# A transformer block with segment memory on one core: token blocks 1 to 3 in one load, a re-annealed instruction list, and other value columns in the memory products of heads 20 to 31

## The chip, the core and the metric

The kernel runs on one core of one Trainium2 chip. The metric is the device time of one execution in microseconds (us). Before the change it is 297.37 us, the median of 3 runs (297.17 to 298.87). One further execution was taken with the profiler; its own time is 295.65 us, of which the profile shows a span of 293.9 us from the first to the last instruction.

The engines have short names here: PE multiplies matrices (PEld loads its weights), ACT evaluates functions and copies, DVE and POOL do elementwise work, and SP issues the transfers (DMAs). Each engine works through its own instructions strictly in order and waits for the others by semaphores.

## The reference

Input `x` has 2048 tokens of 640 features in bf16; there are 32 heads of 20 features and 4 segments of 512 tokens.

```python
def _A_ref(x, wq, wk, wv, wo, beta):          # H = 32, Dh = 20, N = 4, L = 512
    q, k, v = ...                              # x @ wq, x @ wk, x @ wv, cut into heads and segments
    phi = lambda t: jnp.where(t > 0, t + 1.0, jnp.exp(t))
    g = _sigmoid(beta)
    for s in range(N):
        p = _softmax(einsum(qs, ks) * scale + mask)      # causal inside the segment
        a_dot = einsum(p, vs)
        a_mem = einsum(phi(qs), M) / (einsum(phi(qs), z) + 1e-06)
        outs.append(g * a_mem + (1.0 - g) * a_dot)
        M = M + einsum('bhld,bhle->bhde', phi(ks), vs)   # memory: phi(k) of a head times v of the same head
        z = z + einsum('bhld->bhd', phi(ks))
    return o @ wo

h  = x + _A_ref(_layernorm(x), ...)
h2 = h + silu(_layernorm(h) @ w1) @ w2         # w1 640x1728, w2 1728x640
```

## The kernel before

The 2048 tokens are 16 blocks of 128 (numbered 0 to 15), and four blocks are one segment. `build` declares several hundred small tasks for each segment, and each task emits one or a few instructions on one engine. A task's name says what it does. The names that matter later are:

- `x0`, `x1`, `x2`, `x4`, `x8`, `x12`: loads of token blocks by `load_x` (L581), named after their first block; `w_q0`, `w_q1`, `w_k0`, `w_k1`, `w_wv`: the weights of the projections in raw order (L584); `w_wo`, `w_w1_c`, `w_w2_k`: later weights.
- `n1_stB`, `n1_rsB`, `n1_apB`: the first layer norm of block B: statistics on DVE (L753, L756) or on ACT in five instructions (L744 to L748); the reciprocal root on POOL (L763, L765); and the scaling on DVE (L781) or, for block 0, possibly on ACT (L777). For blocks 0 to 3, `n1_tpB` transposes on PE (L791) and `n1_teB` copies the result out on ACT (L800); later blocks are transposed by a DMA (`n1_trB`, L806).
- `re_wqC`, `re_wkC`: copies that put the raw weights of column group C into head order (L711), on DVE, POOL or ACT; group 0 is in two halves, the second one with an `h` at the end.
- `prSCW`: projection of segment S, group C, to q (W=0) or k (W=1) on PE (L548, or L549 for the variant in four column tiles, marked `/C` in the list). `qeSCW` copies it out (L876 on ACT, L877 on DVE). Group 0 of segment 0 is split in token halves x and y.
- `exSCW`, `paSCW`, `pbSCW`: the feature map phi on ACT and DVE (L883, L890, L896).
- `vSB`, `veSB`: the values of a block and their copy (L842 on ACT, L843 on DVE).
- `vtSN`: twelve small DMAs per segment that gather the features of groups 5 to 7 (L908).
- `qkTa`, `qkTb`, `qkTe`: scores of tick T (segment T div 8, head group T mod 8) in PSUM (L946); `eT..` their exponentials on ACT (L959, two for each score task); `mkT..` the causal mask on POOL (L971); `avT` probabilities times values (L994); then `oeT`, `tdT`, `tmT`, `nmT`, `adT` (scaling, transposing, memory read, division, sum).
- `ktSC`, `mzSC`, `mbSC`: the memory update: phi(k) transposed by DMA (L1101), its products with the values (L1112), and the masked copy.
- `otB`, `woB`, `rsB`: attention output transposed, multiplied by `wo`, added to x (L1161, L548, L1176); `n2_...B`: second layer norm; `h1_S_F`, `thS_F`, `sS_F`, `h2_B`, `oB`, `outB`: the feed-forward part (L548/L1198, L1211, L1217, L548, L1254, L1259).

What sets the order is one text, `ORDER`: a list of about 1460 entries, of the form `name/engine:slots`. `Graph.schedule` walks through it, gives each task its engine and its buffer slots (PSUM banks 0 to 7, rotating SBUF buffers), and emits it. So the list fixes the order of work on each engine and on SP's queue. A `Tracker` adds the semaphore waits that the data and the buffers need. Eight PSUM banks are shared by all tasks: a later user of a bank waits for the copy that empties it.

The loads are declared with a first block, a count, a priority and a bandwidth figure; only the first two have an effect on what is emitted:

```python
load_x(0, 1, -100, 2.30, "fix", (SP,))
load_x(1, 1, -99, 2.33, "fix", (SP,))
...
load_x(2, 2, -97, 4.79, "fix", (SP,))
```

A load has one semaphore, so a task that needs any block of a load waits for the whole load.

In the memory update each group C holds heads 4C to 4C+3 in its first 20 rows and parts of heads 20 to 31 in its other rows. One product multiplies phi(k) of such a row block with the values of two or three heads at once, and a mask keeps what belongs together. The masks (`blk_head`) take block 1 to heads 20 to 23, block 3 to heads 24 to 27 and block 5 to heads 28 to 31.

Of the kernel before, what the change touches and what calls it, by code (L numbers as in the profile page):

```python
# [368 lines left out]
qe021/D:0 e0a0 pr010.0:6 vpad2 w_w1_0/S pa021:1 n1_st4:3 pr010.1 qe010/D pa011:2 n1_st5:0 ex011:1 pb011 kt01:3  # L369
qk0b0:4,2 w_w1_2/S e0b2:5 e0b0 v00.0/C:0 pr020.0/C:7 pr020.1/C mk0a qe020/A v00.1/C n1_rs5 vt09:0 zf0 vt03 n1_st7:1  # L370
n1_rs7 qk0e0:2,4 v01.0:6 v01.1 e0e2:2 v02.0:4 e0e0 ve01/D:0 zf1 v02.1 n1_ap5:0 n1_tr5:2 ve00/A vt00 qk1a0:6,1 ex021:1
pr031.0:3 pr031.1 ve02/D n1_st6:7 lsc0 e1a0:1 n1_rs4 n1_ap4:1 e1a2 qe031/D:0 qk1b0:6,4 v03.0:0 lsc1 lsc2 lsc3
pr041.0:2 e1b0:6 pr041.1 x8/S:8,9,10,11 v03.1 e1b2 qe041/D:0 ex031:0 qk2a0:4,6 n1_tr4 mm5 mk0e pa041:2 n1_rs6 n1_ap6:2
n1_tr6 n1_ap7:3 ex041:2 mzc10 mm2 mk0b pr040.0:3 e2a0:3 mta3 pr040.1 pr030.0:2 ve03/D e2a2 qk2b0:4,0 e2b0:0 vt06
pr030.1/C qe040/D pa031:0 av0:3 pb021 mk1a qe030/D mm1 n1_tr7 vt05 oe0/D:0 qk2e0:6,4 vt010 mk1b av1:2 e2b2 epsg1 mk2b
pb041 mk2a td0/C:3 e2e2:5 e2e0 oe1/D:1 qk3a0:4,0 nm0:3,0 vt07 e3a2:6 v10.0:2 td1:6 nm1:2 vt011 e3a0 v10.1 ve10/D:1
qk3b0:0,6 e3b2:4 e3b0 mm7 n1_st9:2 mk2e av2:3 mk3a oe2/D:1 qk4a0:6,4 e4a2:3 v11.0/C:2 e4a0 v11.1/C qk4b0:0,4 td2/C:6
epsg0 ve11/D pb031 mk3b nm2:2 mtb3 av3:7 e4b0:1 vt01 e4b2 vt02 n1_rs9 oe3/D:0 mzc1 n1_st10:7 vt08 n1_st8:1 vt04
qk4e0:2,0 mk4a pr100.0/C:4 e4e2:4 pr100.1/C qe100/D:0 pa100:0 qk5a0:0,6 pr110.0/C:5 pr110.1/C e4e0 qe110/D:0 e5a0:5
w_wo/S:0 qk5b0:2,0 pr120.0/C:4 pr120.1/C qe120/D:0 mk4b e5a2 mk4e av4:5 oe4/D:1 mk5a kt02:0 pa120:0 e5b2:2 qk6a0:0,6  # L380
n1_rs8 td3/C:4 n1_ap8:0 nm3:0 e5b0 mk5b v12.0:2 v12.1 kt04:4 ve12/D e6a0:1 ex120:0 e6a2 w_w2_3/S td4:1 ex100:1 mz01:0
mz00 mm8 mz04 mz02 kt03:1 n1_rs10 n1_ap10:3 mz03 ma0/D:0 qk6b0:4,2 e6b2:0 e6b0 mk6b nm4:3 pr101.0:7 pr101.1 qk6e0:0,2
e6e2:6 qe101/D av5:6 pr111.0/C:7 pr111.1/C e6e0 qk7a0:4,2 mk6e w_w2_0/S mk6a e7a0:4 e7a2 n1_tr8:1 mk7a oe5/D:0 qe111/D
td5:6 pr130.0/C:0 pr130.1/C nm5:1 n1_tr10 qk7b0:6,4 e7b2:5 e7b0 mk7b n1_ap9:0 qe130/D:0 n1_st11:7 v13.0:1 mm3 v13.1/C
ve13/D ex101:2 n1_rs11 av6:0 qk8a0:3,6 e8a0:3 pa101:0 e8a2 pr140.0:5 pr140.1/C av7:4 oe6/D:1 mzc3 qk8b0:0,2 w_w1_4/S
td6/C:6 e8b0:2 w_w1_3/S n1_tr9 mzc5 pb101 kt10:1 qe140/D:0 oe7/D:0 mk8a nm6:2 pr131.0/C:7 td7/C:4 nm7:1 mzc7 mzc4
ot0:0 qk8e0:5,0 pr131.1/C ot1 n1_ap11:1 mm0 qe131/D pr121.0:4 pr121.1 pa130:0 pa110:0 ot2 qe121/D vt19:0 pa131:1 mzc0
e8b2 mk8b e8e0:5 w_w2_4/S mzc2 qk9a0:5,2 pb100 e8e2 mk8e pr141.0:7 pr141.1 qe141/D pa121:0 e9a2:4 qk9b0:0,2 e9a0 pb120
pa111:2 wo0.0/C:4 wo0.1/C rs0 e9b0:6 av8:7 e9b2 vt12 mk9b ot3 ex110:0 wo1.0/C:0 qk10a0:3,5 oe8/D:0 n1_tr11 vt16
n2_st0:1 vt10 e10a0:3 wo1.1 rs1 n2_st1:6 mb00:0 mm11 vt13 e10a2 wo2.0:2 wo2.1 rs2 ex111:2 pb111 n2_st2:0 mk10a  # L390
qk10b0:6,0 e10b2:0 vt11 wo3.0/C:4 wo3.1/C qk10e0:2,0 rs3 vt15 n2_rs1 e10b0 vt14 v21.0:6 e10e2:2 vt18 n2_ap1:0 n2_st3:6
e10e0 v21.1 ve21/D:0 mm9 qk11a0:4,0 e11a0:1 mm6 n2_tr1:0 v20.0/C:2 v20.1/C n2_rs0 v22.0/C:4 n2_rs2 tm8/C:6 td8/C
# [930 lines left out]
```

## Time and profile before

| what | value |
|---|---|
| median of 3 runs | 297.37 us (297.17 to 298.87) |
| the profiled execution's own time | 295.65 us |
| its span | 293.9 us |
| PE busy | 282.0 us (96%), 4365 matmuls |
| DVE, ACT, POOL busy | 218.6, 216.5, 148.1 us |
| chain that ended last, by engine | PE 83%, DVE 7%, ACT 6%, DMA 1%, issue 1% |
| granted PE clock | 9 tenths or more in each slice, mean 1.00 |

Busy time counts instructions on an engine. A share over the whole span mixes stages with different limits: the first 10 us have no projection yet, then scores and exponentials come first, and at the end only the feed-forward part is left. So the table is read together with the views by stretches of time.

### The profile page before, as it was taken

The page shows a single profiled execution, that of the slowest core. Times are in us where ns is not written, and L with a number is a line of the kernel's source. Part 1 is how long each engine was busy: PE and PEld are TensorE (multiplying, and loading weights), DVE is VectorE, ACT ScalarE, POOL GpSimd, SP SyncE. Part 2 cuts the span into 40 slices and gives each one's busy share as a digit, 9 for nine tenths or more (in the row PEclk, how much of TensorE's full clock was granted, in tenths as well). Part 3 has the DMA queues.
Part 4 walks back from the last instruction along what each step waited for, and adds up shares of the span by engine and source line. Part 5 has one row for each costly group of instructions (what it writes and reads, how often), then busy time and mean ns, then how long its engine had stood idle before and what let it go on. Part 6 is the DMA issues. An engine that isn't in the chain of part 4 may idle for free.

```text
span 293.9 us, 10138 instructions
## 1 busy us (share of the span) xinstructions
PE 282.0 (96%) x4365; PEld 159.8 (54%) x4365; DVE 218.6 (74%) x456; ACT 216.5 (74%) x281; POOL 148.1 (50%) x294
## 2 busy tenths in 40 slices
PE   6899889999999999999999899999999999999996
PEld 5454435445644445566654554656664657754574
DVE  3999888899997678798899835877746776635613
ACT  7699999999999899977789857979979640005400
POOL 6759675686947545746748432348638321300000
PEclk9999999999999999999999999999999999999999
DMA  7947869635464200453543402403320031450003
GB/s 212 342 120 186 113 176 186 167 69 108 87 80 113 73 2 3 53 99 70 91 122 92 93 2 21 81 2 57 73 25 2 2 70 22 91 156 0 3 0 112
DMA packets 48604, 24.83 MB, mean 84 GB/s; under 512 B 38896, under 2 KB 47472, under 8 KB 48560
## 3 DMA queue, kind: packets, MB, share of 16 engines
...
## 4 chain that ended last, share of the span: by engine, by line
PE 83%; DVE 7%; ACT 6%; DMA 1%; issue 1%; POOL 0%; SPq 0%; ACTq 0%; DVEq 0%
PE ps_all L548 49%; PE ps_all L549 20%; PE ps_all L946 8%; ACT PT L959 5%; PE ps_all L994 5%; DMA x_tok<-in_A_x_dram 1%; PE ps_all L1198 1%; DVE xn_rot L781 1%; DVE oTs L1010 1%; DVE phiQ L890 1%; DVE stt L753 1%; PE ps_all L1112 1%; DVE Vx L843 1%; DVE otok L1046 1%; DVE QK L877 0%
## 5 line engine op out<-in xcount | busy, mean ns | idle before, releaser
L959 ACT ACTIVATE PT<-ps_all 128x1024 bf16<-128x1024 f32 x160 | 154.1, 1027 | 16.2 <-PE ps_all L946 15.1
L971 POOL TENSOR_SCALAR_AFFINE_SELECT PT<-PT 128x512 bf16<-128x512 bf16 x128 | 82.8, 651 | 63.9 <-ACT PT L959 60.5
L1211 ACT ACTIVATE th<-ps_all 128x512 f32<-128x512 f32 (+1 forms) x56 | 31.7, 589 | 38.1 <-PE ps_all L548 23.7
L1217 DVE SCALAR_TENSOR_TENSOR sT<-th,ps_all 128x512 bf16<-128x512 f32 (+1 forms) x56 | 36.0, 661 | 17.0 <-ACT th L1211 16.4
L548 PE MATMUL ps_all<-w_sb,sT 128*128 128x320 bf16 x324 | 46.3, 299 | 0.1
L548 PE MATMUL ps_all<-tT,w_sb 128*128 128x512 bf16 x178 | 41.4, 380 | 0.0
L548 PEld LDWEIGHTS ps_all<-w_sb,sT 128*128 128x128 bf16 x324 | 31.0, 98 | 13.2 <-issue 0.6
L753 DVE BATCH_NORM_STATS2 stt<-x_tok 128x6 f32<-128x320 bf16 x62 | 27.1, 478 | 3.8 <-DMA x_tok<-in_A_x_dram 3.6
L1072 POOL TENSOR_TENSOR otok<-on 128x320 bf16<-128x320 bf16 x24 | 19.7, 824 | 17.5 <-DVE on L1064 17.5
L1254 DVE SCALAR_TENSOR_TENSOR x_tok<-ps_all,x_tok 128x640 bf16<-128x640 f32 (+1 forms) x17 | 13.3, 784 | 17.9 <-PE ps_all L548 13.1
L548 PEld LDWEIGHTS ps_all<-tT,w_sb 128*128 128x128 bf16 x178 | 16.5, 98 | 18.7 <-issue 0.6
L877 DVE CAST QK<-ps_all 128x512 bf16<-128x512 f32 x25 | 17.1, 685 | 8.6 <-PE ps_all L548 4.7
L1010 DVE TENSOR_SCALAR oTs<-ps_all,lsc 128x512 bf16<-128x512 f32 x26 | 19.3, 741 | 2.6 <-PE ps_all L994 2.2
L549 PE MATMUL ps_all<-tT,w_sb 128*32 128x512 bf16 x328 | 20.5, 380 | 0.0
L1064 DVE TENSOR_TENSOR on<-ps_all,rd 128x640 bf16<-128x640 f32 x24 | 19.8, 824 | 0.8
L765 POOL TENSOR_TENSOR rst<-rst,eps_c 128x1 f32<-128x1 f32 x32 | 18.3, 573 | 2.5
L549 PE MATMUL ps_all<-w_sb,sT 128*32 128x320 bf16 x496 | 18.8, 300 | 0.0
L781 DVE TENSOR_SCALAR xn_rot<-x_tok,mvt,rst 128x640 bf16<-128x640 bf16 x31 | 16.1, 534 | 3.3 <-POOL rst L765 2.8
L548 PE MATMUL ps_all<-tT,wkr 128*128 128x512 bf16 (+1 forms) x77 | 18.4, 367 | 0.0
L548 PE MATMUL ps_all<-wv_sb,tT 128*128 128x320 bf16 x115 | 18.0, 300 | 0.5 <-ACT PT L959 0.3
L763 POOL TENSOR_TENSOR rst<-mvt,eps_c 128x1 f32<-128x1 f32 x32 | 6.7, 209 | 22.5 <-DVE mvt L756 21.8
L994 PE MATMUL ps_all<-PT,Vx 128*32 128x512 bf16 (+3 forms) x384 | 17.4, 301 | 0.0
(111 smaller groups left out, 403.1 us busy)
## 6 DMA issues: line engine op xcount, KB each, us to landing
out_dram<-x_tok SPq DMA_DIRECT2D x15, 160.0 KB, 1.9
...
```

What stands on the lines that cost most here:

```text
L548: return [lambda e: e.matmul(out, lhsT=lhsT, rhs=rhs, start=start, stop=stop)]
L549: return [lambda e, p=p: e.matmul(out[p:p + 32, :], lhsT=lhsT[:, p:p + 32], rhs=rhs, start=start, stop=stop, tile_position=(0, p)) for p i ...
L753: T.add(DV, lambda e, hh=hh: e.bn_stats(out=stt[:, s, 6 * hh:6 * hh + 6], in_=xb[:, 320 * hh:320 * hh + 320]), reads=R((xa, xsub)), writes ...
L946: fns.append(lambda e, j=j, o=o, r=r, q0=q0, q1=q1, qa=qa, ka=ka: e.matmul(ps_all[:, o:o + q1 - q0], lhsT=ka[32 * r:32 * r + DH, 128 * j:1 ...
L959: T.add(AC, lambda e: e.activation(out=pt[:, pta.slot, q0:q0 + 2, 0:width], in_=sc3[:, b0:b0 + 2, 0:width], func=ACT.Exp, scale=SCALE), re ...
L971: fns.append(lambda e, v=v: e.affine_select(out=v, in_=v, pattern=[[0, 4], [1, 128]], compare_op=ALU.is_ge, fill=0.0, base=0, channel_mult ...
L994: fns.append(lambda e, j=j, r=r, h=h, pa=pa, pt=pt, co=co, q0=q0, ji=ji: e.matmul(bank(po)[32 * r:32 * r + 32, q0:hi], lhsT=vtile(vx)[:, j ...
L1010: f = lambda e: e.tensor_scalar(out=o, in0=i_, scalar1=lsc[:, g:g + 1], scalar2=None, op0=ALU.mult)
L1064: T.add(DV, lambda e: e.tensor_tensor(out=on[:, ona.slot, :, :].rearrange("p b (x e) -> p b x e", e=DH), in0=v[:, :, :, 0:DH], in1=r2.unsq ...
L1072: T.add(PO, lambda e: e.tensor_tensor(out=o_dst, in0=on[:, ona.slot, 0, :].rearrange("p (i x) -> p i x", i=4), in1=on[:, ona.slot, 1, :].r ...
L1211: T.add(AC, lambda e: e.activation(out=th[:, tha.slot, lo:hi], in_=bank(ps)[:, lo:hi], func=ACT.Tanh, scale=0.5), reads=R((ps, [0])), writ ...
L1217: T.add(DV, lambda e: e.scalar_tensor_tensor(out=sT[:, f, lo:hi], in0=th[:, tha.slot, lo:hi], scalar=1.0, in1=bank(ps)[:, lo:hi], op0=ALU. ...
```

## The change

There are three edits.

1. Blocks 1, 2 and 3 come in one load of 480 KB instead of one of 160 KB and one of 320 KB; the load `x2` is gone.
2. `ORDER` is another list for the same tasks (less `x2`).
3. In the memory products of groups 0 to 2, the value columns of the second head are 20 heads further on, not 16.

```diff
-    load_x(1, 1, -99, 2.33, "fix", (SP,))
+    load_x(1, 3, -99, 2.33, "fix", (SP,))
     load_w("wv", wv_sb[:, :, :], cw(A_wv), -98, 4.96, [(W["wv"], [0])], "fix", (SP,))
-    load_x(2, 2, -97, 4.79, "fix", (SP,))
...
-                heads = [(4 * c, 16, 2)] if c < 3 else [(12, 8, 3)] if c == 3 else [(16, 8, 2), (28, 1, 1)]
+                heads = [(4 * c, 20, 2)] if c < 3 else [(12, 8, 3)] if c == 3 else [(16, 8, 2), (28, 1, 1)]
```

The list, its first part (old, then new):

```diff
-epsc:0 iota halfc zpad warm:0 x0:0 mt2 n1_st0:4 mt3 mt0 mt1 mta1 mtb1 vpad1 x1:1 n1_st1/A:1,2 x2:2,3 w_q0:0 w_q1 w_k0
-vpad0 fill25:0 n1_rs0 n1_ap0/A:1 sel n1_tp0:2 fill5:7 n1_te0/A:1 n1_st2/D:5,3 mta0 n1_rs1 n1_st3:0 n1_rs2 w_k1 w_wv:0
-n1_rs3 re_wk4/G:0 mtb0 mm4 n1_ap1 n1_tp1:0 n1_ap2 n1_tp2:4 n1_ap3:0 n1_tp3:2 re_wq0/D:0 n1_te1/A pr000x.0:6 re_wq0h/D
-re_wk2/G pr000x.1 re_wk0/D re_wq2/D n1_te2/A n1_te3/A pr001x.0:5 qe000x/D:0 re_wk0h/D pr000y.0:4 re_wq3/G beta
-pr001y.0:0 x4/S:4,5,6,7 pr000y.1 qe000y/A w_w1_1/S:0 mta2 mtb2 mm10 pr001y.1 re_wk1/D re_wq1/D qe001y/A pr001x.1
-pr011.0:2 pr011.1 re_wk3/D qe001x/A re_wq4/G qk0a0:0,3 ex001:0 pa001:0 pb001 kt00:2 pr021.0:7 pr021.1 e0a2:4 qe011/D:0
...
+zpad:0 x0:0 mt0 epsc halfc n1_st0:4 iota sel x1:1,2,3 n1_st2/D:5,3 w_q0:0 w_q1 w_k0 mta0 n1_rs0 fill25:0 warm:0
+n1_st3:0 n1_st1/A:3,0 n1_rs1 w_k1 n1_ap1 n1_ap0/A:1 n1_tp0:2 fill5:7 re_wq0/D:0 n1_rs2 n1_ap2 n1_rs3 n1_tp1:4 n1_tp2:6
+n1_te0/A:0 re_wq0h/G n1_te1/A n1_ap3:2 n1_tp3:1 re_wk0/D:0 n1_te2/A pr000x.0:5 pr000x.1 qe000x/D:0 re_wk0h/G n1_te3/A
+pr001x.0:6 pr000y.0:0 pr000y.1 pr001y.0:4 pr001x.1 pr001y.1 re_wq4/A re_wk1/D qe001y/D qe000y/A re_wk2/D re_wq3/G mtb0
+pr011.0:7 pr011.1 re_wq2/G qe001x/A qk0a0:3,1 ex001:2 qe011/D:0 w_wv:0 beta re_wq1/G w_w2_5/S pa001:0 x4/S:4,5,6,7
+pr021.0:6 pr021.1 qe021/D:0 lsc0 lsc1 e0a2:3 re_wk4/G re_wk3/G w_wo/S:0 pr010.0:7 pr010.1 pb001 n1_st4:3 e0a0 ex011:0
+qk0b0:5,1 n1_rs4 mt2 pr020.0/C:3 qe010/D pr020.1/C mm9 vpad2 qe020/D vt03:0 x8/S:8,9,10,11 e0b2:2 v00.0/C:0 vt06 e0b0
...
```

Read by engine, the lists compare as follows.

- PE has the same 510 tasks in almost the same order: between two neighbouring score tasks stand the same tasks nearly throughout.
- With `/C` stand 30 of 84 `pr` tasks before and 36 after, 9 and 13 of 32 `v`, 33 and 31 of 108 `h1`, 18 and 9 of 65 `h2`, 13 and 8 of 32 `td`, 9 of 24 `tm` and 9 of 32 `wo` both times. The matmuls are 4365 before and 4209 after. Between neighbours in the list PE changes between full array, row tiles and column tiles 173 times before and 176 times after.
- ACT: `qe001y` and `qe020` go to DVE, `re_wq4` comes from POOL, `lsc0` stands ahead of the first exponential, and the load `w_w1_3` is issued from ACT's queue.
- POOL: `re_wq0h`, `re_wk0h`, `re_wq2`, `re_wq1` and `re_wk3` come from DVE; `re_wk2` goes to DVE. The constants `vpad0`, `vpad1`, `mt1`, `mt2`, `mt3` and their masks stand later. The first masks are in the order `mk0e`, `mk1a`, `mk0b`, `mk0a` instead of `mk0a`, `mk0e`, `mk0b`, `mk1a`, `mk1b`.
- DVE: `ve03` stands ahead of `pa041` and `n1_ap6`; `n1_ap8` stands after `ve12`; `n1_ap5` comes after `nm0`, much later than before.
- SP: `x2` is gone; `w_w2_5`, `w_wo` and `x8` come earlier, `kt00` and `kt01` later, and `n1_tr5` is the 27th transfer instead of the 18th (behind `vt08`, `vt07`, `vt010` and `vt00`, among others).
- The last norms of blocks 12 to 15 and the tasks around `wo13` are in another order: 9 PE tasks stand between `wo13.1` and the first `h1_3`, not 14.

More of the change, by code (lines that the diff above doesn't have):

```diff
@@ L368 @@
-pr011.0:2 pr011.1 re_wk3/D qe001x/A re_wq4/G qk0a0:0,3 ex001:0 pa001:0 pb001 kt00:2 pr021.0:7 pr021.1 e0a2:4 qe011/D:0
[L369 to L392, printed above, removed]
@@ new lines @@
+w_w1_2/S:0 n1_rs6 ex021:2 e1a0:6 qe031/D:0 qk1b0:4,6 n1_ap7:0 mm0 w_w1_4/S e1a2 mk1a v03.0:0 pr041.0:2 e1b2:1 mta2
+mtb2 pr041.1 qe041/D:0 mk0b v03.1 ve03/D n1_ap6:2 n1_tr7 e1b0 qk2a0:4,6 mk0a n1_tr6 ex031:0 pr030.0:2 ex041:1 pa041:0
+pr040.0:3 mk1b pr040.1 qe040/D e2a0:0 qk2b0:4,0 pr030.1 e2a2 qe030/D lsc3 e2b0:4 av0:3 vt08 mt1 vt07 e2b2 qk2e0:6,4
+e2e2:2 mm7 vt010 mta1 oe0/D:1 pb041 av1:2 oe1/D:0 mtb1 vt00 td0:3 nm0:2,0 n1_ap5:0 n1_tr5 vt02 mk2b qk3a0:4,0 v10.0:2
+e2e0 td1:7 nm1:0 vt05 v10.1/C ve10/D:1 e3a2:1 n1_st10:4 mt3 e3a0 vt011 pa031:2 pb031 mk2a vt04 qk3b0:0,6 mk2e av2:5
```

160 lines of the change are left out of this document (89 added, 71 removed).

## The prediction

> **What bounds the kernel now.** I read the page's busy line first, then the view of busy time by stretches (span, then PE, PEld, DVE, ACT, POOL, clock, DMA share, GB/s), cut where the limit changes.
>
> ```profile
> PE 282.0 (96%) x4365; PEld 159.8 (54%) x4365; DVE 218.6 (74%) x456; ACT 216.5 (74%) x281; POOL 148.1 (50%) x294
> ```
>
> ```profile
> 0.00:10.05 10.05, 6.45 (x50) 4.56 (x51) 4.94 (x19) 7.28 (x11) 6.51 (x27) 1.00 0.82 258
> 10.05:22.10 12.05, 12.05 (x139) 6.91 (x137) 11.57 (x35) 10.17 (x17) 8.44 (x24) 1.00 0.64 195
> 22.10:58.00 35.90, 32.54 (x608) 16.02 (x608) 31.44 (x68) 34.68 (x41) 24.84 (x51) 1.00 0.84 169
> 58.00:75.00 17.00, 16.43 (x288) 8.36 (x290) 16.39 (x38) 16.22 (x19) 12.45 (x32) 1.00 0.45 82
> 75.00:231.00 156.00, 154.28 (x2864) 86.54 (x2864) 120.05 (x241) 134.73 (x171) 89.86 (x152) 1.00 0.31 58
> 231.00:291.30 60.30, 60.29 (x444) 37.39 (x432) 33.73 (x60) 13.45 (x25) 6.02 (x12) 1.00 0.20 53
> 291.30:293.90 2.60, 0.00 (x0) 0.00 (x0) 0.49 (x1) 0.00 (x0) 0.00 (x0) 1.00 0.21 65
> ```
>
> The reader is to see four regimes. Until 10.05 us PE does only filler products and four transposes: the first load and norms set the pace. From 10.05 to 22.10 PE is busy without a gap (12.05 of 12.05). From 22.10 to 58 ACT is the limit: 34.68 of 35.90 us, while PE idles 3.36 us. From 58 to 75 both are nearly full. From 75 to 291.3 PE is the limit (154.28 of 156, then 60.29 of 60.30). The granted clock is 1.00 in each. So PE work is a fixed sum, and the end moves with what delays PE at the start, what ACT loses between 22 and 75 us, and any new hole in PE after that. Time saved on another engine after 75 us buys nothing.
>
> **The start before, step by step** (timelines: start, duration, what). The chain begins at the loads:
>
> ```profile
> 0.80 1.35 SPq L581 DMA_DIRECT2D x_tok<-in_A_x_dram  x3
> 3.59 0.74 ACT L744 ACTIVATE xn_rot<-x_tok 128x640 bf16<-128x640 bf16 x1 [0.23 <-DMA x_tok<-in_A_x_dram]
> 5.42 0.19 ACT L748 ACTIVATION_READ_ACCUMULATOR xn_rot<-x_tok,stt 128x1 f32 x1
> 5.61 0.92 ACT L777 ACTIVATE xn_rot<-x_tok,nmr,rst 128x640 bf16<-128x640 bf16 x1
> 7.07 0.70 ACT L800 ACTIVATE tT<-ps_all 128x640 bf16<-128x640 f32 x1 [0.55 <-PE ps_all L791]
> 8.90 2.02 ACT L800 ACTIVATE tT<-ps_all 128x640 bf16<-128x640 f32 x3 [1.13 <-PE ps_all L791]
> 12.06 0.94 ACT L876 ACTIVATE w_sb<-ps_all 128x256 bf16<-128x256 f32 x3 [1.14 <-PE ps_all L548]
> 13.92 1.94 ACT L959 ACTIVATE PT<-ps_all 128x1024 bf16<-128x1024 f32 x2 [0.26 <-PE ps_all L946]
> ...
> 1.72 4.14 DMA x_tok<-in_A_x_dram
> ...
> 5.88 0.88 DVE L753 BATCH_NORM_STATS2 stt<-x_tok 128x6 f32<-128x320 bf16 x2 [1.56 <-DMA x_tok<-in_A_x_dram]
> 7.79 0.21 DVE L756 BATCH_NORM_AGGREGATE mvt<-stt 128x2 f32<-128x12 f32 x1
> 9.22 0.45 DVE L781 TENSOR_SCALAR xn_rot<-x_tok,mvt,rst 128x640 bf16<-128x640 bf16 x1 [0.51 <-POOL rst L765]
> 10.31 0.40 DVE L711 COPY wqr<-sT 128x400 bf16<-128x400 bf16 x2
> 10.82 0.42 DVE L877 CAST w_sb<-ps_all 128x256 bf16<-128x256 f32 x1
> ...
> 5.71 0.19 POOL L763 TENSOR_TENSOR rst<-mvt,eps_c 128x1 f32<-128x1 f32 x1
> 5.97 0.55 POOL L765 TENSOR_TENSOR rst<-rst,eps_c 128x1 f32<-128x1 f32 x1
> 10.45 1.06 POOL L711 COPY wkr<-sT 128x400 bf16<-128x400 bf16 x3 [1.33 <-DMA sT<-in_A_wk_dram]
> ...
> 10.08 0.71 PE L548 MATMUL ps_all<-tT,wqr 128*128 128x256 bf16 x5
> 13.47 0.39 PE L946 MATMUL ps_all<-w_sb 20*128 20x512 bf16 x4
> ```
>
> Block 1 alone reaches ACT at 3.59, and ACT does its five statistics instructions until 5.61 and the scaling of block 0 (L777) until 6.53, all while blocks 2 and 3 are still under way: they land 4.14 us after their issue at 1.72, at 5.86. From 5.86 the chain is DVE statistics, POOL, DVE, PE, ACT; PE's first projection starts at 10.08, the first score product (`qk0a0`) at 13.47, the first exponential at 13.92.
>
> **The change at the start.** Let L be the time at which the one load of blocks 1 to 3 lands. ACT's order is unchanged: `n1_st1`, `n1_ap0`, `n1_te0`... So `n1_st1` now waits for 480 KB instead of 160 KB, and behind it on ACT wait the scaling of block 0, its transposes on PE, and everything after. Step by step, with the durations above:
>
> - ACT statistics of block 1: 3.59 to 5.61 is 2.02, so L+2.04. Scaling of block 0: 0.92, so L+2.96. Its transposes and the wait until L800: 7.07 less 6.53 is 0.54, so `n1_te0` runs from L+3.50 to L+4.20.
> - POOL's root for block 1 (5.71 to 6.52, 0.8) now comes ahead of those of blocks 2 and 3, so these end at L+2.96, L+3.78 and L+4.60. DVE follows 0.1 later with 0.45 each: `n1_ap3` ends at L+5.15, its transposes allow PE's first projection at about L+5.55 (before: 10.08 − 5.86 = 4.22 after the landing).
> - ACT copies four blocks in a row at 0.70: `n1_te1` starts at L+4.50 (the filler products come between), `n1_te3` ends at L+6.60. The y half of the projection needs it and starts at L+6.65. Five pieces, about 1.3 us, and one full projection of five products, 1.08, follow: `qk0a0` at L+9.13, the first exponential 0.45 later.
> - In front of that stand on ACT `re_wq4` (new there) and two copies. ACT shows no copy of this kind: three instructions of between 0.20 and 0.63 us each, the nearest ACT rows here being the copies L876 (three within 0.94) and L800 (0.70 for 640 columns), make 0.6 to 1.9; I take 1.0. ACT would then be done at L+8.4, while the DVE copy of the last piece (0.42) ends at L+8.55: hidden. At 1.9 it would add 0.6.
>
> **L itself.** The trace shows no load of three blocks. These rows bound it (KB each, median us to landing):
>
> ```profile
> x_tok<-in_A_x_dram SPq DMA_DIRECT2D x2, 160.0 KB, 2.3
> x_tok<-in_A_x_dram SPq DMA_DIRECT2D x1, 320.0 KB, 4.1
> ```
>
> The issue stays at about 1.26, the second of the three in 1.35 us. From below: as fast as one block, 1.26 + 2.3 = 3.6. From above: 1.8 more for each further block, as between these rows, 1.26 + 2.3 + 3.6 = 7.2. Nearest is the sum of the two loads that it replaces: the same bytes in the same queue, landed at 5.86, and the last of them now issued one issue (0.45) earlier. I take 5.6. Then `qk0a0` is at 14.73, **1.26 late** (at L = 3.6, where the key weights, whose landing ended POOL's wait before 10.45, begin to bind, at most 0.7 is gained; at 7.2 it is 2.9 late).
>
> [...]
>
> From 10.05 to 22.10 PE has no gap, so PE carries the delay to the second tick: the list has the same PE tasks up to there. `qe020`, which leaves ACT, and DVE's lighter load give nothing back in this stretch.
>
> **The ACT-bound stretch (22 to 75 us).**
>
> ```profile
> 28.21 0.81 DVE L843 CAST sT<-ps_all 128x640 bf16<-128x640 f32 x1
> 29.16 0.40 PE L946 MATMUL ps_all<-w_sb 20*128 20x384 bf16 x8 [0.35 <-DVE sT L843]
> 29.61 8.66 ACT L959 ACTIVATE PT<-ps_all 128x1024 bf16<-128x1024 f32 x9 [0.42 <-PE ps_all L946]
> 49.65 0.40 PE L946 MATMUL ps_all<-QKV 20*128 20x384 bf16 x8 [0.33 <-DVE Vx L843]
> 50.10 1.02 ACT L959 ACTIVATE PT<-ps_all 128x1024 bf16<-128x1024 f32 x1 [0.66 <-PE ps_all L946]
> ...
> 25.76 1.34 POOL L971 TENSOR_SCALAR_AFFINE_SELECT PT<-PT 128x512 bf16<-128x512 bf16 x2
> 27.36 0.74 POOL L971 TENSOR_SCALAR_AFFINE_SELECT PT<-PT 128x512 bf16<-128x512 bf16 x1
> ...
> tT<-xn_rot SPq DMA_TRANSPOSE x28, 2.7
> ```
>
> - ACT's holes of 0.42 and 0.66 come from PSUM banks that DVE emptied late (`ve03` behind `pa041` and two scalings; `ve12` behind `n1_ap8`). The new list puts both copies earlier: I take **−0.35 and −0.5** (bounds 0 and the whole hole).
> - POOL gets five groups of weight copies, about 1 us each by the row at 10.45, for two that leave. Its first masks slip: `mk0e`, `mk1a`, `mk0b`, `mk0a` end near L+25.7, where `av0` could start at L+24.9. `av0` holds `qk2e0` behind it on PE, and so ACT; the later masks of ticks 1 and 2 repeat it. **+0.45** (0 if POOL catches up in its idle 11 of 35.9 us; the bound above is the first rival).
> - `n1_tr5` waits on SP behind four gathers, and its input `n1_ap5` behind `nm0` on DVE: issued near 35.6, 2.7 to land, 38.3, where `v11.0` on PE is due at 38.5. The slowest gathers and transposes here took longer: 0 to 1.5, **+0.3**.
>
> **The rest costs nothing or little.** The three more changes of PE's array shape fall before 58 us, beside PE's 3.36 idle. Memory products: the same count and shapes, only other columns. The late constants on POOL stand in its idle half. The issue of `w_w1_3` on ACT (0.5 at most, as on SP) meets PE-bound time. In the last norms DVE has statistics, scaling and root of blocks 12 to 15 in a row behind `wo12.1`; I count them to 0.2 us before the first `h1_3`, where they had 14 tasks of cover before and now 9: 0 to 0.5, **+0.1**. After 75 us PE's order and the distances between producers and users in the list are as before: 0, bounded by −1.7 (all of PE's idle time there) and as much again above.
>
> **Sum.** 1.26 − 0.35 − 0.5 + 0.45 + 0.3 + 0.1 = +1.26, taken as +1.3. The profiled execution took 295.65 for a span of 293.9; the new one would take 296.95. The median of the runs lies 1.7 above the profiled one, so on its scale the time is 297.37 + 1.3 = **298.7**. A measurement of this kernel can tell about 1% (3 us) from no change.
>
> **Rivals.**
>
> 1. *POOL becomes the bound in ticks 0 to 4 (slower).* If the weight copies on POOL run as the slowest of them do beside DVE, each mask from `mk0e` on is late, each late mask holds an `av`, the score product behind it, and ACT. Its work between 10 and 27 us is nearly gapless in the new order (17 us); 20% longer is 3.4 us, less the 0.45 counted: +4.2 in all, 301.6. It decides when POOL loses more than 1 us to its neighbours. For it: 24.84 of 35.9 us busy already, and five more copies. Against: idle time further on, where it can catch up.
> [...]
> 3. *The list removes the holes (faster).* With an early load and ACT's 1.22 and 0.78 and PE's 1.72 idle of the stretches gone: −3.7, 293.7. For it: no hole is needed by the sums of work. Against: the distances in the list are the same.
>
> **How the numbers follow.** Forecast 0.50, with its own range 297.5 to 300.5 from L between 5.0 and 6.2 and the holes; a tenth of it lies over 1%. Rival 1 0.30, early load 0.10, rival 3 0.10. Faster by over 1% (below 294.4): 0.10. Slower by over 1% (above 300.3): 0.30 and 0.05, 0.35. The rest 0.55. The range of 295.0 to 302.5 takes in the early load and most of rival 1.
>
> **What would show it.** Right: the load of 480 KB lands near 5.6; ACT's L744 starts there, L777 ends about 3 us later; PE's first projection at 11.1 and the first exponential near 15.2 (13.92 before); ACT idle between 23 and 59 us not above 1.2; the stretch before the end without a hole. Wrong: ACT's first statistics before 4.5; POOL without a gap up to 35 us and waits of PE (L994) for POOL masks over 2 us in all; a hole before the first `h1_3`.

## The result and the profile after

The kernel after takes 302.01 us (median of 6 runs, 300.89 to 303.40) beside 298.12 us for the kernel before: a ratio of 1.0142, 95% interval 1.0100 to 1.0184. A second measurement of the same pair (run e12 below) gave 300.68 beside 297.48 us, ratio 1.0104 (1.0064 to 1.0144). The ratios are those on record, which are not quite the quotients of the two medians. So the change costs 1.0 to 1.4%, 3 to 4 us. The forecast was 298.7 us with a range of 295.0 to 302.5: the range holds, the likeliest case's own range (297.5 to 300.5) does not.

The profiled execution took 302.03 us for a span of 300.3. That is 6.4 us more than the profiled one of before (293.9), which ran below its median; where the traces are compared, 6.4 us have to be explained, of which some 2 are that choice of execution.

The page's busy line and the granted clock by slice:

```profile
PE 285.3 (95%) x4209; PEld 160.5 (53%) x4209; DVE 218.9 (73%) x449; ACT 217.0 (72%) x282; POOL 148.9 (50%) x300
...
PEclk9799999999999999999999999999999999999999
```

The same stretches as before the change (columns: span, its length, then PE, PEld, DVE, ACT, POOL, clock, DMA share, GB/s):

```profile
0.00:10.05 10.05, 6.86 (x43) 4.98 (x44) 4.56 (x15) 6.14 (x10) 4.30 (x18) 0.95 0.83 271
10.05:22.10 12.05, 11.70 (x133) 6.84 (x131) 9.09 (x24) 9.67 (x18) 8.01 (x26) 0.90 0.56 169
22.10:58.00 35.90, 32.75 (x595) 15.70 (x597) 32.82 (x74) 34.59 (x41) 28.14 (x61) 1.00 0.68 127
58.00:75.00 17.00, 16.52 (x303) 8.32 (x293) 15.41 (x31) 16.42 (x20) 11.72 (x29) 1.00 0.44 76
75.00:231.00 156.00, 150.82 (x2590) 84.02 (x2591) 118.65 (x238) 131.23 (x167) 84.98 (x149) 1.00 0.41 72
231.00:291.30 60.30, 60.30 (x517) 36.30 (x518) 34.98 (x64) 18.97 (x32) 11.73 (x21) 1.00 0.21 39
291.30:300.30 9.00, 6.35 (x47) 4.35 (x45) 3.37 (x5) 0.00 (x0) 0.00 (x0) 1.00 0.21 73
```

Two rows carry the news. Between 10 and 22 us PE is busy for 11.70 of 12.05 us, but at a granted clock of 0.90, where it was 1.00. And between 75 and 231 us PE idles 5.2 of 156 us, where it idled 1.7: in the stretch that the prediction put at nothing.

How the shift grows is read from the starts of score products in the timelines of PE. For ticks 12, 13, 23 and 24 they stand, before the change, at

```profile
82.24 0.40 PE L946 MATMUL ps_all<-QK 20*128 20x512 bf16 x4
...
91.23 0.40 PE L946 MATMUL ps_all<-QKV 20*128 20x512 bf16 x4
...
164.50 0.40 PE L946 MATMUL ps_all<-QKV 20*128 20x512 bf16 x4
...
176.94 0.40 PE L946 MATMUL ps_all<-QK 20*128 20x512 bf16 x4
```

and after it at

```profile
84.19 0.39 PE L945 MATMUL ps_all<-QK 20*128 20x512 bf16 x4
...
95.15 0.39 PE L945 MATMUL ps_all<-QKV 20*128 20x512 bf16 x4
...
170.11 0.40 PE L945 MATMUL ps_all<-QKV 20*128 20x512 bf16 x4 [0.35 <-ACT Vx L841]
...
183.31 0.40 PE L945 MATMUL ps_all<-QK 20*128 20x512 bf16 x4
```

The shift is +1.95 us at tick 12 (1.78 of it stands already at the first exponential), +3.92 at tick 13, +5.61 at tick 23, +6.37 at tick 24, and then constant to the end. So there are four places: the start, 84 to 92 us, 126 to 170 us, and 174 us. Of the 4.4 us that come after tick 12, 3.4 are idle time of PE; the other 1.0 lies in its busy time (by the view of stretches between the same score products, 9.41, 73.27 and 11.48 us where it was 8.99, 72.70 and 11.43), and what that is was not followed.

**The start** (timeline of after):

```profile
5.38 0.74 ACT L743 ACTIVATE xn_rot<-x_tok 128x640 bf16<-128x640 bf16 x1 [2.00 <-DMA x_tok<-in_A_x_dram]
7.30 0.91 ACT L776 ACTIVATE xn_rot<-x_tok,nmr,rst 128x640 bf16<-128x640 bf16 x1
15.70 1.02 ACT L958 ACTIVATE PT<-ps_all 128x1024 bf16<-128x1024 f32 x1 [0.15 <-PE ps_all L945]
...
8.26 0.45 PE L790 MATMUL ps_all<-ident,xn_rot 128*128 128x128 bf16 x5 [2.06 <-ACT xn_rot L776]
11.37 1.23 PE L548 MATMUL ps_all<-tT,wqr 128*128 128x256 bf16 x5
```

ACT's first statistics wait for the load of 480 KB until 5.38 (3.59 before), and the scaling of block 0, which needs nothing of that load, stands behind them. PE waits 2.06 us for it (1.14 before). The first projection then takes 1.23 us for five products of the kind that took 0.71 before: half the clock, and the record of after grants 0.50 from 9.02 to 12.43 us. The first exponential starts 1.78 us late; the landing and its chain are 1.0 to 1.1 of it and the clock 0.6 to 0.8 (0.6 beside e5 below, 0.8 beside the prediction's chain).

**84 to 92 us.** Timeline of ACT before:

```profile
81.69 0.71 ACT L842 ACTIVATE Vx<-ps_all 128x640 bf16<-128x640 f32 x1
```

Timeline of DVE, then PE, after:

```profile
83.19 0.73 DVE L895 TENSOR_TENSOR phiQ<-phiQ,ex 128x512 bf16<-128x512 bf16 x1
83.84 1.01 DVE L895 TENSOR_TENSOR phiK<-phiK,ex 128x512 bf16<-128x512 bf16 x1
84.77 0.81 DVE L842 CAST Vx<-ps_all 128x640 bf16<-128x640 f32 x1
85.50 0.67 DVE L876 CAST QK<-ps_all 128x512 bf16<-128x512 f32 x1
...
85.64 0.33 PE L548 MATMUL ps_all<-Mzb,phiQ 128*128 128x84 bf16 x4 [1.06 <-DVE Vx L842]
```

`ve23`, the copy of the last values of segment 2, was done by ACT as soon as `v23` ended (81.69 before). The new list gives it to DVE behind `pb110` and `pb111`, and `tm9` needs its bank. That wait is 1.06 of the 1.97 us that this place adds; 0.33 more are a wait for a gather at 92.24, and the rest is in gaps too short to be listed and in PE's busy time.

**126 to 174 us.** Timelines of DVE and PE before:

```profile
155.79 0.89 DVE L753 BATCH_NORM_STATS2 stt<-x_tok 128x6 f32<-128x320 bf16 x2
...
168.80 0.23 PE L946 MATMUL ps_all<-QKV 20*128 20x128 bf16 x3 [0.88 <-issue]
```

Timeline of DVE (first row) and PE after:

```profile
161.75 0.89 DVE L752 BATCH_NORM_STATS2 stt<-x_tok 128x6 f32<-128x320 bf16 x2 [1.66 <-DMA x_tok<-in_A_x_dram]
...
128.75 0.67 PE L993 MATMUL ps_all<-PT,Vx 128*32 128x512 bf16 x12 [0.62 <-issue]
164.48 0.73 PE L993 MATMUL ps_all<-PT,Vx 128*32 128x512 bf16 x16 [0.65 <-DVE sT L1216]
174.03 1.05 PE L549 MATMUL ps_all<-tT,w_sb 128*32 128x512 bf16 x16 [1.72 <-issue]
```

DVE waits 1.66 us for blocks 12 to 15. Their load overwrites blocks 0 to 3 and goes out when `out3` has landed, at 155.87 (151.26 before), which is only 0.4 us more than the shift of 4.2 that PE has by then; but it lands 5.9 us after its issue, not 4.5. Six traces with the new list have 5.5 to 6.7 us for this load, six with the old list (before, e1, e4, e8, e10, e11) 4.3 to 4.6. The new list puts transposes of phi(k) right ahead of it and two right behind it on SP; that they are what slows it was not tested. Behind that wait DVE empties a bank late, and `av21` waits 0.65; the shift grows by 1.4 us from the first scores of tick 22 to those of tick 23. The two rows with "issue" wait for nothing that the profile shows; before, the view of waits has one such wait of 0.9 us in this range, so that the two add 0.3 and 0.8 us to the shift. What they are is the subject of e5 and e6.

### The profile page after: what moved, and what is told of

The parts are those of the page before. It is cut to its first block, busy times and chain, and to the rows that moved or that the text cites. A ratio compares the mean times of both kernels' runs of the same rounds, so it can differ in the third digit from the quotient of the medians.

```text
span 300.3 us, 9825 instructions
## 1 busy us (share of the span) xinstructions
PE 285.3 (95%) x4209; PEld 160.5 (53%) x4209; DVE 218.9 (73%) x449; ACT 217.0 (72%) x282; POOL 148.9 (50%) x300
## 4 chain that ended last, share of the span: by engine, by line
PE 71%; DVE 14%; DMA 7%; SPq 2%; issue 2%; ACT 2%; POOL 1%; DVEq 0%; ACTq 0%
PE ps_all L548 46%; PE ps_all L549 13%; PE ps_all L945 6%; PE ps_all L993 4%; DMA x_tok<-in_A_x_dram 3%; DVE stt L752 2%; SPq L907 2%; DVE oTs L1009 2%; DVE xn_rot L780 1%; DVE QK L876 1%; DVE phiK L895 1%; ACT PT L958 1%; DMA phiKt<-phiK 1%; PE ps_all L1111 1%; DVE otok L1045 1%
## 5 line engine op out<-in xcount | busy, mean ns | idle before, releaser
L548 PE MATMUL ps_all<-w_sb,sT 128*128 128x320 bf16 x386 | 55.8, 299 | 0.0
L548 PEld LDWEIGHTS ps_all<-w_sb,sT 128*128 128x128 bf16 x386 | 36.8, 98 | 16.0 <-issue 1.5
L548 PE MATMUL ps_all<-tT,w_sb 128*128 128x512 bf16 x183 | 43.0, 379 | 0.1
L549 PE MATMUL ps_all<-tT,w_sb 128*32 128x512 bf16 x308 | 18.9, 380 | 1.7 <-issue 1.7
L548 PE MATMUL ps_all<-tT,wkr 128*128 128x512 bf16 (+1 forms) x73 | 17.4, 365 | 0.2
L882 ACT ACTIVATE ex<-QK 128x512 bf16<-128x512 bf16 x25 | 15.4, 632 | 0.7 <-DVE phiK L895 0.7
L945 PE MATMUL ps_all<-QK 20*128 20x512 bf16 (+3 forms) x240 | 15.1, 301 | 0.6 <-DMA QKV<-QK 0.3
```

The source lines that it names most:

```text
L548: return [lambda e: e.matmul(out, lhsT=lhsT, rhs=rhs, start=start, stop=stop)]
L549: return [lambda e, p=p: e.matmul(out[p:p + 32, :], lhsT=lhsT[:, p:p + 32], rhs=rhs, start=start, stop=stop, tile_position=(0, p)) for p i ...
L945: fns.append(lambda e, j=j, o=o, r=r, q0=q0, q1=q1, qa=qa, ka=ka: e.matmul(ps_all[:, o:o + q1 - q0], lhsT=ka[32 * r:32 * r + DH, 128 * j:1 ...
```

## The experiments

Times are medians; each ratio is against the kernel before, which took 297.28 us beside e1 to e4, 297.72 beside e5 to e8 and 297.48 beside e9 to e12 (three chips, so that ratios are what is compared between these groups).

**e1: the load alone.**

```diff
-load_x(1, 1, ...)  load_x(2, 2, ...)     x1:1 n1_st1/A:1,2 x2:2,3
+load_x(1, 3, ...)                        x1:1,2,3 n1_st1/A:1,2
```

> The list of before with the one load of 480 KB put in (x1:1,2,3 ahead of n1_st1, x2 gone), the value columns as before. Theory 1 (the late landing and a half-speed clock behind it delay the whole start, and nothing gives it back): ACT's first statistics start near 5.4 us instead of 3.59, the first exponential +1.0 to +1.8 us against 13.92 (+1.0 if the granted clock stays 1.00 between 9 and 12.5 us, +1.8 if it falls to about 0.5 there), and the same +1.0 to +1.8 us at the end. Theory 2 (the cost is the list's, the load is hidden behind blocks 2 and 3, which come at 5.86 anyhow): first exponential within 0.3 us of 13.92 and the time within 0.5 us of before.

298.24 us, ratio 1.0037 (1.0015 to 1.0059): +1.0 us. Timeline of ACT:

```profile
5.16 0.74 ACT L743 ACTIVATE xn_rot<-x_tok 128x640 bf16<-128x640 bf16 x1 [1.79 <-DMA x_tok<-in_A_x_dram]
...
15.83 1.02 ACT L958 ACTIVATE PT<-ps_all 128x1024 bf16<-128x1024 f32 x1 [0.26 <-PE ps_all L945]
```

Theory 1 holds: the first exponential is 1.91 us late (clock 0.71 between 10 and 15 us in this execution), the load is not hidden, and in the median 1.0 us remains.

**e2: the list alone.**

```diff
-load_x(1, 3, ...)                        x1:1,2,3
+load_x(1, 1, ...)  load_x(2, 2, ...)     x1:1 x2:2,3
```

> The kernel after with block 1 in a load of 160 KB and blocks 2 and 3 in one of 320 KB again; list (but for x2) and value columns as after. Theory 1: ACT's first statistics at 3.6 us, first exponential near 13.9 us (15.70 after), clock 1.00 throughout, time 1.8 us below the kernel after (300.2) and about 2 to 3 us above before, because the list's later stalls (the values copied late at 84 us, the late load of blocks 12 to 15, instruction fetches) stay. Theory 2 (the load costs nothing): the time of the kernel after, 302.0. Theory 3 (the load is the whole loss): the time of before, 298.

300.62 us, ratio 1.0118 (1.0063 to 1.0173): +3.3 us. Timeline of ACT:

```profile
3.63 0.74 ACT L744 ACTIVATE xn_rot<-x_tok 128x640 bf16<-128x640 bf16 x1 [0.25 <-DMA x_tok<-in_A_x_dram]
...
13.90 1.94 ACT L959 ACTIVATE PT<-ps_all 128x1024 bf16<-128x1024 f32 x2 [0.15 <-PE ps_all L946]
```

The first exponential is back at 13.90 (13.92 before), so the start's loss belongs to the load, and the list by itself loses nothing there. But the larger part of the loss stays: it is the list's (this kernel keeps the value columns of after too, which cost nothing, as e4 shows). The two parts, 0.4 and 1.2%, make 1.6% beside the 1.0 to 1.4% of the whole, which is within the intervals.

**e4: the value columns alone.**

```diff
-heads = [(4 * c, 16, 2)] if c < 3 ...
+heads = [(4 * c, 20, 2)] if c < 3 ...
```

> The kernel before with the other value columns alone (stride 20 heads instead of 16 in the memory products of groups 0 to 2). Same count and shapes of products, other columns of the same tile: every theory expects 0.0 us, within 0.5. The use of the run: a second profile of the order of before, which shows how far the waits without a visible releaser (PE held 0.45 us and 1.10 us with '<-issue' near 132 and 168 us in before's profile) and the granted clock vary from one execution to the next. Theory 1 (these waits belong to the place in the program where the instruction stream crosses a fetched piece): they stand at the same instructions with the same lengths within 0.3 us. Theory 2 (they depend on what the transfers do at that moment): lengths differ by more than 0.5 us.

296.84 us, ratio 0.9989 (0.9954 to 1.0023): no difference. Its trace has PE's wait without a releaser at the same product as before's (1.1 us, 0.9 before), and one of 0.5 us near 100 us that before's trace lacks. So most of such a wait belongs to the place, and about half a microsecond comes and goes.

**e3: the late copy at 84 us.**

```diff
-v23.0:4 v23.1 pb110 ... pb111 ... ve23/D tm9
+v23.0:4 v23.1 ve23/D pb110 ... pb111 ... tm9
```

> The kernel after with one entry moved: ve23 (values of block 11, on DVE) right behind v23.1, ahead of pb110 and pb111, so that its bank is free 1.7 us earlier. Theory 1 (PE waits for that bank: the 1.06 us idle before the memory read at 85.64): that wait is gone and the time falls by 1.1 to 2.0 us, to 300 to 301. Theory 2 (the delay is only handed on: pb110 and pb111 come 0.9 us later on DVE, and with them oe9, tm9 or the first h1, so PE waits there instead): the sum of PE's waits between 83 and 92 us stays within 0.4 us and the time within 0.4 us of 302.0.

301.37 us, ratio 1.0141 (1.0102 to 1.0181): no gain that the times show. Timeline of DVE (first row) and PE:

```profile
82.58 0.83 DVE L842 CAST Vx<-ps_all 128x640 bf16<-128x640 f32 x1
...
85.38 1.25 PE L548 MATMUL ps_all<-tT,wkr 128*128 128x512 bf16 x5 [0.89 <-DVE QK L876]
```

The wait ahead of `tm9` is gone, and `pr211` waits 0.89 us for the next copy, `qe201`, which still stands behind `pb111`. Theory 2: the delay is handed on.

**e7: blocks 12 and 13 in a load of their own.**

```diff
-load_x(12, 4, ...)                       ... out3 ... x12/S
+load_x(12, 2, ...)  load_x(14, 2, ...)   ... x12/S out3 ... x14/S
```

> The kernel after with blocks 12 and 13 in a load of their own, issued ahead of out3 (near 152.5 us instead of 155.9), and blocks 14 and 15 where the load of four stood. Theory 1 (DVE waits 1.66 us for the four blocks, and behind it s1_5_0 and s1_4_0 free PE's banks late): the load of 12 and 13 lands before 157, DVE does not wait for it, PE's 0.82 us before av21 are gone, time 0.8 to 1.2 us less, 301. Theory 2 (the gain is given back: PE comes to the fetched piece at 171.6 earlier and waits there as much longer): shift at the tick-23 scores -0.8 us, but at the end within 0.3 of 302.

300.88 us, ratio 1.0130 (1.0091 to 1.0168). Timelines of SP, DVE and PE:

```profile
154.32 0.40 SPq L581 DMA_DIRECT2D x_tok<-in_A_x_dram  x1
...
161.56 0.88 DVE L752 BATCH_NORM_STATS2 stt<-x_tok 128x6 f32<-128x320 bf16 x2
...
165.21 0.72 PE L993 MATMUL ps_all<-PT,Vx 128*32 128x512 bf16 x16
```

Both waits are gone, and from tick 22 to tick 23 this trace wins 1.4 us on that of after. The time doesn't show it: the ratio lies between the two of after (1.0142 and 1.0104). In the same trace a gather of the first segment held PE for 1.87 us at 43 us (0.93 in after), and the granted clock is 0.50 from 44.23 to 47.64 us, right behind that wait, which hides the gain in that one execution.

**e5: more filler products ahead of the first transposes.**

```diff
-fill25:0
+fill40:0
```

> The kernel after with 40 filler products instead of 25 ahead of the first transposes (fill25:0 becomes fill40:0), so that PE idles about 0.4 us before them instead of 2.06. Theory 1 (the 2 us of idle let the granted clock fall to 0.5 for 3.4 us, in all six runs of the kernel after and in most of the merged load's, and that costs 0.8 us): the granted clock is 1.00 from 5 us on, the first score product is 0.7 to 0.8 us after the same point of the load (9.9 us behind the landing becomes 9.1), time 301.2. Theory 2 (the clock falls for the phase of its window, not for the idle): clock 0.5 in some window before 13 us as before, time 302.0. Theory 3 (the filler is too long where the first stretch runs at half clock): the transposes of block 0 wait for the filler and the start comes 0.3 us later still.

302.04 us, ratio 1.0143 (1.0099 to 1.0186): no gain in the median, although the profiled execution took 299.32. The trace does show what was asked: by the view of stretches its clock is 1.00 between 5 and 10 and between 10 and 15 us, and the first score product comes at 14.39, 9.23 us behind ACT's first statistics (5.16), not 9.87. So the chain of the prediction (9.13 from the landing) was right at full clock. Of the six runs five have a mean clock of 0.999 or 1.0; of the six of after none has (three of six in e12).

It showed something else as well. Timeline of PE, where after waits 1.72 us:

```profile
167.03 1.53 PE L548 MATMUL ps_all<-wv_sb,tT 128*128 128x320 bf16 x10 [1.02 <-DMA tT<-xn_rot]
...
170.68 1.27 PE L549 MATMUL ps_all<-tT,w_sb 128*32 128x512 bf16 x20
```

Fifteen products more at the start, and the wait inside `h1_1_11` is gone. The page's third part lists 33 transfers of kind "instruction" on queue q8 after the change; 4209 matmuls and 4209 weight loads over 33 are 255 each (4365 and 4365 over 34 are 257 before), so these look like pieces of PE's own instructions. In the trace of after one of them goes out at 171.55 us, amid column tiles, and PE stops at 172.3 until 174.03. In e5 one goes out at 164.92, under products of the full array, and the only stop of PE behind it up to 172 us, 1.02 us at 167.03, is put down by the profile to a transposed norm. That these are pieces of PE's stream is borne out by a count in the traces: in after, e2, e3, e9 and e12 the wait at 172 to 176 us stands behind the same number of recorded instructions of PE's stream, PEld's among them (5825), and so do those of before, e1, e4, e10 and e11, where other tasks stand at that count; the wait at 126 to 132 us in after, e2, e3, e9 and e12 stands 1536 instructions ahead of it, six times 256.

**e6: fewer column tiles.**

```diff
-h2_0_0/C h2_0_1/C tm16/C td16/C h2_0_2/C wo4.0/C ... h1_1_7/C h1_1_6/C ... h1_1_11/C
+h2_0_0   h2_0_1   tm16   td16   h2_0_2   wo4.0   ... h1_1_7   h1_1_6   ... h1_1_11
```

> The kernel after with ten entries in the full array instead of in four column tiles (h2_0_0, h2_0_1, h2_0_2, tm16, td16 and wo4.0 ahead of 129 us; the h1_1_6, h1_1_7 and h1_1_11 pieces ahead of 174 us), so that PE issues a quarter of the matmuls for the same work there. Theory 1 (PE runs out of instructions: a fetched piece of 16 KB holds some 120 matmuls, and column tiles use them up four times as fast): the two waits without a releaser (1.0 us before av17 ends, 1.9 us inside h1_1_11) shrink below 0.5 us each; time 1.5 to 2 us less, 300.2, of which up to 0.5 is lost to more changes of the array's shape. Theory 2 (a wait stands at each boundary of a fetched piece whatever runs there): they move to other tasks with the same sum of 2.9 us, time 302.

300.12 us, ratio 1.0092 (1.0055 to 1.0128). Timeline of PE:

```profile
150.38 0.29 PE L945 MATMUL ps_all<-QK 20*128 20x256 bf16 x4 [1.09 <-issue]
...
174.75 0.40 PE L945 MATMUL ps_all<-QKV 20*128 20x384 bf16 x8 [0.74 <-issue]
```

Of the two places that were put into the full array, the wait at 129 us is gone, and the 1.72 us inside `h1_1_11` have become 0.74 behind it, ahead of the next scores. The other row, 1.09 us at 150 us, is new: nothing was changed there but which piece begins, and fourteen products of the full array stand right ahead of it. Both theories are half right: the waits at the two places shrink, and moving the boundaries makes a new one. Nor do column tiles alone make the wait. In the traces PE goes on 2.1 to 2.9 us after the transfer of a piece goes out (1.65 in the new one here), so that its wait is what is left of this time when its earlier instructions are done (in after the transfer goes out at 171.55, PE's work ends at 172.3 and goes on at 174.03); what decides when the transfer goes out is not shown. The median is the lowest of all kernels with the whole change, by 0.6 to 1.9 us; against e12 that isn't separated.

**e8: the prediction's two copies, in the kernel before.**

```diff
-v03.1 e1b2 qe041/D ... pa041 n1_ap6 n1_ap7 ... ve03/D     n1_ap8 nm3 ... ve12/D
+v03.1 ve03/D e1b2 qe041/D ... pa041 n1_ap6 n1_ap7 ...     nm3 ... ve12/D n1_ap8
```

> The kernel before with two copies on DVE earlier, as the new list has them: ve03 right behind v03.1 (ahead of pa041 and two scalings of norms), and n1_ap8 behind ve12. Theory 1 (the prediction's two terms): ACT's waits of 0.42 us at 29.6 and 0.66 us at 50.1 are gone, shift -0.35 at tick 3 and -0.85 at tick 7, time 0.85 us less than before. Theory 2 (the work of DVE that is put off is late next): the shift at tick 3 comes as predicted but av2's copy, pa041 or the transposed norms of block 8 then hold PE by as much; time within 0.3 us of before.

297.86 us, ratio 1.0019 (0.9990 to 1.0048). Timeline of ACT (first row) and PE:

```profile
28.54 0.63 ACT L883 ACTIVATE ex<-w_sb 128x512 bf16<-128x512 bf16 x1 [1.32 <-DVE w_sb L877]
...
30.13 0.40 PE L946 MATMUL ps_all<-w_sb 20*128 20x384 bf16 x8 [0.75 <-ACT PT L959]
```

`ve12` gives what was said: ACT's wait of 0.66 is gone and the shift falls by 0.46 between ticks 6 and 7. `ve03` was put too far forward: it waits on DVE for its product with `qe041` behind it, ACT's `ex041` waits 1.32 us for that, and the scores that should come sooner come 0.87 later.

**e10: a shorter filler, in the kernel before.**

```diff
-fill25:0
+fill14:0
```

> The kernel before with 14 filler products instead of 25 ahead of the first transposes, so that PE idles about 2.3 us there instead of 1.14; the loads and all else as before. Nothing waits for the filler, so the time can change through the clock (and the place of the fetched pieces, 11 matmuls earlier) alone. Theory 1 (idle of 2 us in the window lets the clock fall): granted clock 0.994 or less in most of the runs (6 of 23 for before), in the profile 0.5 for 3.4 us between 8 and 13 us, first exponential 0.5 to 0.9 us later, median +0.5 to +1.5 us. Theory 2 (the phase of the window decides, not the idle): the same share of runs at 0.994 as before, median within 0.5 us.

298.39 us, ratio 1.0033 (1.0002 to 1.0064). Timeline of PE:

```profile
6.59 0.71 PE L791 MATMUL ps_all<-ident,xn_rot 128*128 128x128 bf16 x5 [2.30 <-ACT xn_rot L777]
7.10 1.27 PE L620 MATMUL ps_all<-zpad 128*128 128x256 bf16 x5
```

The five transposes take 0.71 us (0.45 before) and the five fillers 1.27 (0.71): the times that they have in e12 at a granted clock of 0.50, here from the start to 10.3 us. Yet the first exponential comes at 13.84, no later than before, as other waits cover it up to 10 us. The median is 0.9 us higher all the same; what that is, this trace, of a run of 297.16 us, doesn't show. The granted clock of those stretches and the run's mean clock are nevertheless given as 1.00, so that this count is no measure here, and only 3 of 12 runs have a lowered one. Theory 1 as written fails in the trace: with a longer idle PE stays at that pace, but the first exponential was late only where the low stretch fell on the projections after 10 us, as in after (9.0 to 12.4 us).

**e12: the kernel after again.**

```diff
 (no edit)
```

> The kernel after, unchanged, on the same chip as the three others, for a second trace. Theory 1 (all that was found belongs to the list and the load): ACT's first statistics near 5.3 us, the clock at 0.5 in most runs, PE's waits of 1.0 to 1.1 us before tm9, 1.0 to 1.2 us near 129 us, 0.8 us before av21 and 1.7 to 2.1 us inside h1_1_11 again; time 301.5 to 302.3. Theory 2 (part of it was that one execution): one of these waits is missing or below half its length, and the time differs by as much.

300.68 us, ratio 1.0104 (1.0064 to 1.0144). Timelines of ACT, DVE and PE:

```profile
4.95 0.74 ACT L743 ACTIVATE xn_rot<-x_tok 128x640 bf16<-128x640 bf16 x1 [1.59 <-DMA x_tok<-in_A_x_dram]
15.08 1.94 ACT L958 ACTIVATE PT<-ps_all 128x1024 bf16<-128x1024 f32 x2 [0.15 <-PE ps_all L945]
...
160.52 0.89 DVE L752 BATCH_NORM_STATS2 stt<-x_tok 128x6 f32<-128x320 bf16 x2 [1.38 <-DMA x_tok<-in_A_x_dram]
...
85.00 0.33 PE L548 MATMUL ps_all<-Mzb,phiQ 128*128 128x84 bf16 x4 [1.10 <-DVE Vx L842]
172.95 1.05 PE L549 MATMUL ps_all<-tT,w_sb 128*32 128x512 bf16 x16 [1.91 <-issue]
```

Every place stands again at nearly its length; the start loses 1.16 us here in place of 1.78, as the load lands 0.4 earlier and the stretch at half clock ends at 10.98 us, not at 12.43. The time is 1 us below the expected 301.5, though no wait is missing. Theory 1, with that reserve.

**e9: after with three places put right.**

```diff
-x1:1,2,3 | ve23/D ... pb111 ex131 ... qe201/D ... e12a0         | out3 ... x12/S (4 blocks)
+x1:1 x2  | ve23/A ...             ... qe201/D pb111 ... e12a0 ex131 | x12/S (2) out3 ... x14/S (2)
```

> The kernel after with three places put right at once: block 1 in its own load again; ve23 on ACT behind e11b0, with qe201 ahead of pb111 on DVE and ex131 behind e12a0 on ACT; blocks 12 and 13 in a load of their own ahead of out3. Theory 1 (the loss is these three places and what the fetched pieces add): start -1.8 us, 84 to 92 us -1.5 to -2.0, tick 23 -1.2, together -4.5 to -5.0: time 297 to 297.5, that of before, though the waits for instructions (3 us in all) are still there. Theory 2 (the places are not additive, each gain is spent at the next wait): at most -2.5 us, time 299.5 or more.

299.10 us, ratio 1.0061 (1.0034 to 1.0088). Its profiled execution took 303.63 us, with the clock at half between 9.0 and 15.8 us and from 90.9 to 94.3, right behind the wait shown here, and serves for the order of waits alone. Timeline of PE:

```profile
90.29 1.72 PE L548 MATMUL ps_all<-tT,w_sb 128*128 128x512 bf16 x5 [2.00 <-DMA tT<-xn_rot]
```

By the ratios 1.3 to 2.4 us of the loss are recovered, not 4.5 to 5: nearer to its second theory. With the copies in time, the first feed-forward product of segment 0 waits 2.00 us for the transposed second norm: in the new list the last scalings of that norm end on DVE at 81.6 and 83.3 us in the trace of after (the last at 79.7 before), and `n2_tr3` and `n2_tr2` go out on SP at 82.9 and 85.1 (the last two at 79.0 and 80.3 before; 86.2 and 87.5 in e9). In after the last one landed at 87.8, just before that product at 87.86. So three delays lay on top of each other at 84 to 92 us, and removing one or two shows the next.

**e11: before, with what the runs point to.**

```diff
-fill25:0 ... pa041 n1_ap6 ... ve03/D     n1_ap8 nm3 ... ve12/D
+fill33:0 ... pa041 ve03/D n1_ap6 ...     nm3 ... ve12/D n1_ap8
```

> The kernel before with what the runs point to: n1_ap8 behind ve12 on DVE (it gave 0.46 us), ve03 behind pa041 and ahead of the two scalings (so that qe041 and ex041 are not held), and 33 filler products instead of 25. Expected if the sums of the earlier runs hold: -0.46 and -0.35 us, and fewer runs at a lowered clock (worth 2 us in one run of four): median 1.0 to 1.3 us below before, 296.2. If the ACT-bound stretch gives its holes back elsewhere, or the filler delays the transposes: within 0.3 us of before.

297.24 us beside 297.48, ratio 0.9988 (0.9959 to 1.0017): no difference shown. In its trace both holes of ACT are smaller (shift −0.25 at tick 3, −0.46 at tick 7), and then PE meets a new wait. Timeline of PE:

```profile
169.83 0.24 PE L994 MATMUL ps_all<-PT,Vx 128*32 128x128 bf16 x3 [1.52 <-issue]
```

Eight filler products more move the place where 5825 instructions of PE's stream are done, and it falls into `av22`. What the copies win is lost: the shift against before's trace goes from −0.45 behind tick 7 to +0.33 at tick 21, ahead of this wait, and to +1.37 behind it. No kernel of this study beats the one before beyond doubt.

## Why the prediction was right or wrong

- **The landing, L.** Taken 5.6, measured 5.35 and 4.9 (ACT starts at 5.38 and 4.95): the size was right within its bounds. No run shows a load of 480 KB that lands so early that nothing is lost, the case with 0.10 of the chances, which rival 3 and the range take in too: in after, e1, e3, e5 and e12 ACT's first statistics start between 4.95 and 5.38 us, and the first exponential is 1.16 to 1.91 us late in after, e1 and e12.
- **The chain behind it, L + 9.13.** Right at full clock (e5: 9.23; its terms as written add up to 9.03, and 0.1 is not named). It failed by 0.6 to 0.8 us where the clock was granted at half, which the prediction's rows, all at 1.00, did not price. In the trace of after the granted clock is 0.50 for 3.41 us (9.02 to 12.43), behind 3.41 us at 1.00 in which PE idles for 2.06 us. Before the kernel's end the kept traces have eight such falls to half, at the start and behind the waits at 43 us (e7) and 90 us (e9), each behind 3.41 us with 1.8 to 2.1 us of idle time; two other stretches of that length, with 1.8 (e7, at the start) and 1.9 us of it (e2, at 170 us), were not followed by one, so the idle time alone doesn't decide it.
- **The two holes.** −0.35 and −0.5 predicted; in after the shift falls from 1.78 to 1.25 between the first and last scores of tick 2, and by 0.51 from tick 6 to tick 7. Right. Some 0.2 of the first fall is in the traces of e1 and e4 too, which have the old order there, so that 0.35 of it is the list's.
- **POOL (+0.45, and rival 1).** PE waits for a POOL mask once between 22 and 58 us, 0.2 us. Rival 1 gave 301.6, close to the measured time, but its mechanism is not in the trace. So it is luck that the stated range holds the time: its upper part was there for this rival.
- **`n1_tr5` (+0.3).** Its place was right: in after `v11.0` waits 0.65 us for it. A gather of the first segment, not counted, holds the scores of tick 4 for 0.93 besides.
- **The last norms (+0.1).** No hole: PE is busy 60.30 of 60.30 us from 231 to 291.3.
- **"After 75 us PE's order and the distances between producers and users in the list are as before: 0".** This is the step that failed, worth 4.4 us in the traces: some 2.0 at 84 to 92 us, 1.4 at the load of blocks 12 to 15, and 1.1 at the two waits for instructions. PE's order is as before, but what feeds it is not. `ve23` goes from ACT to DVE, behind two phi tasks. The comparison by engine ahead of the prediction leaves that out, with 13 other tasks that change engine, 11 of them after 75 us (`ve31`, `ve32` and `ve33` among them). DVE ends the last scaling of the second norm 3.6 us later, 1.7 more than the shift up to there. The load of blocks 12 to 15 takes 1.4 us longer to land. The first two could be read from the list, by comparing the position of each producer within its own engine's sequence; the landing and the pieces of instructions could not. The bound of "as much again above" 1.7 was too small.

So the forecast was +1.3 us and the result is +3.2 to +3.9; of the difference up to 0.5 us is the start, and most of the rest that one term. By time, e1 and e2 show how the loss divides between load and list; within the list the waits are read from traces, only the repair of three places at once (e9, the load among them) lies clear of the first measurement of after, and the loss of 0.6% that it leaves is not taken apart.
